# Cosine attention and a low-rank mixer MLP: buffer fills ahead of their loads, score bursts of two for one batch, one more PSUM bank

## The chip, the cores and the metric

The kernel runs on one core of a Trainium2 chip. The metric is the device time of one execution in microseconds (us). The kernel before takes 595.03 us, the median of three runs (594.52 to 596.84). The profiled execution that the views below describe has a span of 594.7 us.

## What is computed

Cosine attention over 8 batches, 12 heads, 448 tokens and 64 features per head, and then a mixer over each batch of 448 x 768: a low-rank mix along the tokens (rank 32), a residual, and an MLP from 768 to 3072 and back, with a second residual. In the reference, cut to what matters:

```python
q_n = q / (norm(q) + 1e-06);  k_n = k / (norm(k) + 1e-06)
scores = (q_n @ k_n.T) / tau
attn = softmax(scores)                      # over the keys
x = (attn @ v), heads side by side          # [8, 448, 768]
u = x + (x.transpose(0, 2, 1) @ U @ V).transpose(0, 2, 1)
out = u + relu(u @ w_ch1) @ w_ch2
```

## The kernel before, in words

**Stages of one batch.** Attention and MLP of all batches are woven into one stream. For each batch: GpSimd loads q and k in three thirds of four heads (`load_qk`, L490) and v (`load_v`, L510 for batches 0 to 2, L513 and L518 for the others). VectorE takes squares, sums and normalises (`stats`, `norm`, L540, L544, L612). The result xn is transposed to qkT: on the matrix engine (PE) for batches 0 and 1, by a transposing DMA from the sync queue for the others (L627). PE forms scores (`scores`, L670), ScalarE takes the exponential into attn (L688), PE multiplies with v (`values`, L713), and VectorE divides by the sum, which comes out of a column of ones beside v (L720, L722). `stage0` makes the low-rank mix (L768, L815) and adds it to X to give u (L829). u is transposed to uT (by DMA from batch 2 on, L849), and `mlp` runs the up product (L891), the relu (L914 on ScalarE or L916 on VectorE), the down product (L927), the residual (L938) and the store (L952).

**Buffers.** There are two v buffers, `v_t`, used by even and odd batches. Up to batch 2 (`b < WIDE`, 3) keys lie in four chunks of 112 rows; from batch 3 on in chunks of 128, with the last 64 keys of two pairs of heads sharing the 128 rows of the fourth chunk. So each v buffer has to be filled anew once, with ones beside v and zeros in the half that a head does not use: `set_v_tiles` (L976), five memsets on VectorE (L978, and L980 and L981 twice). `v_set[b]` holds that fill. It can start when the products with v of the batch that used the buffer before are done (`last_av`), and the products of the new batch wait for it. attn has three buffers, xn three, qkT six, u eight tiles, uT one, and the q/k tiles three.

**PSUM.** The eight banks are shared by rings, each with an ordered list of banks and a cap on how many it may hold: `r_sc` (scores, pairs of banks 0 to 5), `r_av` and `r_av2` (products with v), `r_low` (mixer products), `r_mm`, `r_up`, `r_out` (MLP products).

**Order.** A planner in the kernel's Python (`Plan`) simulates the five engines with a cost for each operation and writes out one fixed order for each engine. PE and GpSimd take operations from streams: PE prefers transposes, then products with v, the mixer, scores, and MLP products last; GpSimd has a single stream, so its loads keep the order in which they are written. VectorE, ScalarE and the sync queue take the ready operation with the lowest `prio`. DMAs have an estimated latency `lat`: a number, or a queue ("in" for loads, "x" for transposes) with a work and a fixed part. In the finished order each engine runs its instructions in turn and waits on semaphores where data or buffers demand it.

**Bursts.** `BURST[b]` says how many score slots (a pair of heads, a chunk of keys) of batch b are issued together. A burst of more than two slots is `big`: PSUM banks 0 to 5 are kept for it while it is next and its inputs are ready, and it is tied into the MLP of an earlier batch. Batch 2's big bursts are tied to the up products 0, 3, 6, ... 21 of batch 1; those of batch b from 3 on to down products of batch b - 2 (`SPOTS`). Batches 0 and 1 have no such ties. `BURST[b] > 2` also chooses the rings: `r_av2` rather than `r_av` in `values` (L708), `r_low` rather than `r_mm` in `stage0` (L758).

Of the kernel before, what the change touches and what calls it, by code (L numbers as in the profile page):

```python
# [269 lines left out]
def kernel(  # L270
# [14 lines left out]
    B, H, S, D = q.shape  # L285
# [3 lines left out]
    NPAIR = H // 2  # L289
# [7 lines left out]
    EPS = 1e-6  # L297
    PE_BATCHES = 2
    LATE, VLATE = 8.0, 2.8
    BURST = [1] + [2] * 1 + [3] * 6  # L300
    SPOTS = {8: [(6,)] * 7 + [()], 6: [(5, 17), (10,), (6,), (6,), (6,), (6,)]}
    WIDE = 3
    RAW_KEYS = {(0, 0), (0, 1), (0, 2), (0, 3)}
# [8 lines left out]
    def fixed(n, shape, dt, name):  # L312

        tiles = [const.tile(shape, dt, name=f"{name}{i}") for i in range(n)]
        return tiles
# [11 lines left out]
    v_t = fixed(2, [128, H, SC, D + 2], BF, "v_nat")  # L327
# [38 lines left out]
    def bank_ring(groups, cap, shape=None):  # L366
        def make(g):
            if len(g) > 1:
                return bank_t[:, g[0]:g[-1] + 1, :]
            t_ = bank_t[:, g[0], :]  # L370
            if shape is not None:
                t_ = t_[:, 0:shape[0] * shape[1]].rearrange("p (a b) -> p a b", a=shape[0])
            return t_
        return BankRing(banks, groups, cap, make)
# [2 lines left out]
    r_av = bank_ring([(5,), (6,), (7,), (4,)], 2, (4, D + 8))  # L377
    r_sc = bank_ring([(0, 1), (2, 3), (4, 5)], 3)
    r_low = bank_ring([(5,), (4,), (3,), (2,), (1,), (0,)], 2)
    r_av2 = bank_ring([(5,), (4,), (3,), (2,), (1,), (0,)], 2, (4, D + 8))  # L380
    r_up = bank_ring([(7,), (6,), (5,), (4,), (3,), (2,), (1,), (0,)], 4)
    r_out = bank_ring([(7,), (6,), (5,), (4,)], 4)
    r_warm = bank_ring([(4,)], 1)
# [18 lines left out]
    def rows(ap, c, s0, s1):  # L402

        return ap.rearrange("(s c) d -> c s d", c=SC)[c, s0:s1]
# [13 lines left out]
    def pe_t(n):  # L418
        return n / 2400.0 + 0.0025
# [4 lines left out]
    def dve_t(n, fast=1, fixed=0.065):  # L424
        return fixed + n * 0.00105 / fast
# [4 lines left out]
    def load(fn, busy, deps=(), acq=(), rel=(), late=2.0):  # L430
        return plan.add(Op("POOL", 0.71, fn, deps=deps, acq=acq, rel=rel,
                           lat=("in", busy, late)), pool_q)

    def fill(fn, n=256, prio=8, acq=(), deps=()):
        return plan.add(Op("DVE", 0.05 + n * 0.0005, fn, deps=deps, acq=acq, prio=prio))
# [47 lines left out]
    last_av = {}  # L483
# [12 lines left out]
    def key_rows(n0, n1):  # L496
        n = n0
        while n < n1:
            j, r = divmod(n, 128)
            c, s_ = divmod(n, SCH)  # L500
            m = min(n1 - n, 128 - r, SCH - s_)
            yield j, r, c, s_, s_ + m
            n += m

    def load_v(b):

        old = [last_av.get((b - 2, p)) for p in range(NPAIR)]
        src = v[b].rearrange("h (s c) d -> c s h d", c=SC)
        if b < WIDE:
            ops = [load(lambda c=c: nc.gpsimd.dma_start(out=v_t[b % 2][0:SCH, :, c, 0:D], in_=src[c]),  # L510
                        SCH * H * 0.001, deps=old, late=LATE if b else VLATE) for c in range(SC)]
        else:
            ops = [load(lambda j=j, r0=r0, c=c, s0=s0, s1=s1: nc.gpsimd.dma_start(  # L513
                out=v_t[b % 2][r0:r0 + s1 - s0, :, j, 0:D], in_=src[c, s0:s1]),
                (s1 - s0) * H * 0.001, deps=old, late=LATE) for j, r0, c, s0, s1 in key_rows(0, 384)]
            (_, _, c, s0, s1), = key_rows(384, S)
            for e, hh in ((0, 0), (0, 1), (1, 0), (1, 1)):
                ops.append(load(lambda e=e, hh=hh, c=c, s0=s0, s1=s1: nc.gpsimd.dma_start(  # L518
                    out=v_t[b % 2][64 * e:64 * e + 64, 2 * e + hh::4, SC - 1, 0:D],
                    in_=src[c, s0:s1, 2 * e + hh::4]),  # L520
                    (s1 - s0) * H * 0.00025, deps=old, late=LATE))
        for h in range(H):
            got[b, h, "v"] = ops
# [169 lines left out]
    def values(b, p, X):  # L693
# [12 lines left out]
        for hh in range(2):  # L706
            h = 2 * p + hh
            av, rd = Slot(r_av2 if BURST[b] > 2 else r_av, 1), Slot(r_rd, 1)  # L708
            for t in range(4):
# [46 lines left out]
    def stage0(b, X, muls):  # L756
        par = b % 2
        bank = r_sc1 if b == 1 else r_low if BURST[b] > 2 else r_mm  # L758
        by_pe = b < PE_BATCHES
# [110 lines left out]
    def mlp(b, us, uT, ut):  # L870
# [28 lines left out]
        for f in range(NC):  # L899
# [5 lines left out]
            if b == 0 and 9 <= f < 21 and f % 2:  # L905
                by_tokens(us, *state["first"], (f - 9) // 2)
            mm = early[f]
            o = up(f, mm, range(CC - 1, CC) if b == 0 and f < AHEAD else range(CC))
            r = Op("ACT/DVE", any_t(n), None, deps=[o], acq=[relu], rel=[mm],
                   prio=0)  # L910
# [10 lines left out]
        for group in groups:  # L921
            mms = [Slot(r_out if b == 0 else r_mm, 1) for _ in group]
            last, line = {}, []
            for f in range(NC):
                for (i, t, c0, c1), mm in zip(group, mms):
                    last[mm] = plan.add(Op("PE", pe_t(c1 - c0), lambda i=i, f=f, c0=c0, c1=c1, mm=mm:
                        nc.tensor.matmul(  # L927
                            out=mm.tile[:, 0:c1 - c0], lhsT=relu.tile[:, f, i * 128:(i + 1) * 128],
                            rhs=w2_t[:, f, c0:c1], start=(f == 0), stop=(f == NC - 1)),
                        deps=[done[f], w2_ops[f * len(w2_ops) // NC]],  # L930
                        acq=[mm] if f == 0 else [], rel=[relu] if f == NC - 1 else []), pe_mlp)
                    line.append(last[mm])
            downs.append(line)
            for (i, t, c0, c1), mm in zip(group, mms):
                w = c1 - c0
                O = Slot(r_O, 0)
                o = plan.add(Op("DVE", dve_t(w), lambda i=i, c0=c0, c1=c1, w=w, mm=mm, O=O:
                    nc.vector.tensor_add(out=O.tile[:, 0:w], in0=mm.tile[:, 0:w],  # L938
                                         in1=us[i].tile[:, c0:c1]),
                    deps=[last[mm]] + got.get((b, "u"), []), acq=[O], rel=[mm, us[i]], prio=1))  # L940
                for bb in (b - par, b - par + 1):
                    o0 = (bb % 2) * S
                    lo, hi = max(128 * t, o0), min(128 * (t + 1), o0 + S)
                    if lo >= hi:
                        continue
                    for nn, j, p0, p1 in segments(lo - o0, hi - o0):
                        r0 = nn + o0 - 128 * t
                        by = "ACT" if w < CH and p1 - p0 < SCH else "SP"
                        O.uses += 1
                        O.left += 1  # L950
                        plan.add(Op(by, 0.1, lambda bb=bb, j=j, p0=p0, p1=p1, r0=r0, O=O, c0=c0, c1=c1, by=by:
                            (nc.scalar if by == "ACT" else nc.sync).dma_start(  # L952
                                out=rows(out[bb], j, p0, p1)[:, c0:c1],
                                in_=O.tile[r0:r0 + p1 - p0, 0:c1 - c0]),
                            deps=[o], rel=[O], prio=2, lat=4.0))

        todo = bursts.get(b + 2, ()) if b else ()
        for o, f in zip(bursts.get(2, ()) if b == 1 else (), [0,3,6,9,12,15,18,21]):
# [17 lines left out]
    def set_v_tiles(t_):  # L976
        x = t_.rearrange("p (g e h) c d -> p g e h c d", e=2, h=2)
        nc.vector.memset(t_[:, :, 0:SC - 1, D:D + 2].bitcast(mybir.dt.uint32), ones)  # L978
        for e in range(2):
            nc.vector.memset(x[64 * e:64 * e + 64, :, e, :, SC - 1, D:D + 2].bitcast(mybir.dt.uint32), ones)  # L980
            nc.vector.memset(x[64 * e:64 * e + 64, :, 1 - e, :, SC - 1, :].bitcast(mybir.dt.uint32), 0)  # L981
# [33 lines left out]
    def groups_of(b):  # L1015
        if b < WIDE:
            slots = [(p, c) for p in range(NPAIR) for c in range(SC)]
            return [slots[n:n + BURST[b]] for n in range(0, len(slots), BURST[b])]
        slots = []
        for p in range(0, NPAIR, 2):  # L1020
            slots += [(p, 0), (p, 1), (p, 2), (p + 1, 0), (p + 1, 1), (p + 1, 2), (p, 3)]
        return [slots[n:n + BURST[b]] for n in range(0, len(slots), BURST[b])]

# [5 lines left out]
    def att(b):  # L1029
        X = Slot(r_X, 0) if b else X0  # L1030
        muls = [] if b else list(muls0)
        for x in groups_of(b) if b else ():
            scores(b, x)
        for p in range(0 if b else 1, NPAIR):
            if b == 0:
                for c in range(SC):
                    scores(b, [(p, c)])
            muls += values(b, p, X)
        if b < WIDE <= b + 2:
            v_set[b + 2] = [fill(lambda: set_v_tiles(v_t[b % 2]), 1200, prio=5, deps=[last_av[b, p] for p in range(NPAIR)])]  # L1040
        else:
            v_set[b + 2] = v_set[b]
        last_mul.extend(muls)
        return stage0(b, X, muls)
# [9 lines left out]
    v_set = {0: [fill(lambda: set_v(v_t[0]), 1000, prio=-1.4)]}  # L1054
    begun = stats_first(*first)
    X0 = Slot(r_X, 0)
    for c in range(SC):
# [7 lines left out]
                      deps=[zf, *begun], prio=-2, lat=12.0)) for t in range(4)]  # L1065
# [82 lines left out]
```

## Time and profile before

Busy time of three engines in stretches of the span, in us, with the clock that PE was granted, from the trace:

| stretch (us) | PE busy | VectorE busy | ScalarE busy | PE clock |
|---|---|---|---|---|
| 60 to 90 | 30.00 | 18.21 | 18.00 | 1.00 |
| 90 to 120 | 29.84 | 28.76 | 12.82 | 1.00 |
| 120 to 150 | 25.39 | 22.73 | 16.25 | 0.94 |
| 150 to 180 | 29.94 | 25.52 | 15.36 | 1.00 |
| 180 to 210 | 27.74 | 21.24 | 9.86 | 1.00 |
| 210 to 240 | 30.00 | 20.16 | 16.44 | 1.00 |
| 510 to 540 | 29.89 | 2.82 | 4.78 | 1.00 |

A stretch is 30 us long, so what is missing from 30 in the PE column is time in which no matmul ran. Attention work thins out to the right: VectorE is hardly busy near the end, where only MLP products are left. A row "waiter <- releaser: total, times, longest" in the view of waits says how long an engine stood before an instruction and what let it go; in a timeline the same stands in square brackets. Of the kernel's 384 score matmuls and 1536 products with v, those of batch 2 are found between 110 and 175 us.

### The profile page before, as it was taken

To read this page: it belongs to the slowest core of one execution; us is meant where nothing else is said; L and a number is where in the kernel's file an instruction comes from. 1 tells how busy PE (TensorE), PEld (TensorE's weight loads), DVE (VectorE), ACT (ScalarE), POOL (GpSimd) and SP (SyncE) were. 2 spreads that over 40 slices of the span, in tenths; PEclk is the share of its full clock that TensorE was granted. 3 is DMA by queue.
4 is the path that set the end of the run, shared out by engine and by line. 5 is a ranking of instruction groups with operands and counts; after the bars stand their busy time and mean duration, and the time that the engine had idled before them with its cause. 6 is when DMAs were issued, how large, how long until landed. Compare 5 with 4: busy or idle time off the path is not lost.

```text
span 594.7 us, 11669 instructions
## 1 busy us (share of the span) xinstructions
PE 577.5 (97%) x4860; PEld 329.2 (55%) x4878; DVE 300.9 (51%) x724; ACT 268.9 (45%) x445; POOL 89.8 (15%) x128
## 2 busy tenths in 40 slices
PE   7999999996999899999999999999999999999997
PEld 5555656543556565554456665654455666654565
DVE  7869849996986758466714671244202241110011
ACT  6977743563543364445454345335453444014300
POOL 8234220161024014013200040000000000000000
PEclk9999999998999999999999999999999999999999
DMA  9999992897739849356734690422021100310021
GB/s 155 199 207 192 209 138 69 136 106 88 116 41 165 102 63 109 90 107 79 62 67 83 102 99 21 105 59 45 0 55 41 40 15 1 94 40 1 1 53 54
DMA packets 133332, 50.68 MB, mean 85 GB/s; under 512 B 98208, under 2 KB 133280, under 8 KB 133280
## 3 DMA queue, kind: packets, MB, share of 16 engines
q0 software_dynamic: 72160, 25.73, 39.2%
q1 hardware_dynamic: 61056, 24.19, 20.0%
q8 instruction: 38, 0.62, 0.4%
q14 instruction: 14, 0.11, 0.1%
q10 hardware_dynamic: 64, 0.02, 0.0%
HBM read 52.25 MB, written 11.01 MB: 106 GB/s over the span
## 4 chain that ended last, share of the span: by engine, by line
PE 89%; DMA 4%; ACT 2%; DVE 2%; issue 1%; POOL 0%; DVEq 0%; ACTq 0%; POOLq 0%
PE bank L927 36%; PE bank L891 35%; PE bank L713 8%; PE bank L670 7%; DMA v_nat<-in_v_dram 2%; ACT attn L683 2%; PE bank L815 2%; DMA uT<-u_nat 1%; PE bank L468 1%; DMA qk_nat<-in_k_dram 1%; DVE xn L612 1%; PE bank L768 1%; DVE X_sb L722 0%; POOL qk_nat L490 0%; ACT sq L538 0%
## 5 line engine op out<-in xcount | busy, mean ns | idle before, releaser
L891 PE MATMUL bank<-uT,w_sb 128*128 128x384 bf16 (+1 forms) x1135 | 230.8, 353 | 8.3 <-DVE relu L916 4.3
L927 PE MATMUL bank<-w_sb,relu 128*128 128x384 bf16 (+1 forms) x1368 | 231.2, 323 | 0.0
L688 ACT ACTIVATE attn<-bank 128x896 bf16<-128x896 f32 (+1 forms) x161 | 137.1, 922 | 109.6 <-PE bank L670 109.5
L927 PEld LDWEIGHTS <-relu 128*128 128x128 bf16 x1368 | 128.4, 98 | 90.2 <-issue 12.3
L891 PEld LDWEIGHTS <-w_sb 128*128 128x128 bf16 x1152 | 109.7, 98 | 110.8 <-issue 16.2
L914 ACT ACTIVATE relu<-bank 128x384 bf16<-128x384 f32 (+1 forms) x164 | 88.8, 542 | 154.9 <-PE bank L891 153.5
L938 DVE TENSOR_TENSOR O_sb<-bank,u_nat 128x384 f32<-128x384 f32 (+1 forms) x57 | 31.0, 547 | 178.4 <-PE bank L927 156.3
L544 DVE TENSOR_REDUCE ss<-sq 112x8 f32<-112x512 bf16 x96 | 63.1, 673 | 1.3 <-ACT sq L538 1.1
L713 PEld LDWEIGHTS <-attn 128*128 128x128 bf16 (+1 forms) x1536 | 55.9, 98 | 10.2 <-issue 3.3
L713 PE MATMUL bank<-v_nat,attn 128*128 128x65 bf16 (+1 forms) x1536 | 58.9, 194 | 0.1
L612 DVE TENSOR_TENSOR xn<-qk_nat,inv 112x512 bf16<-112x512 bf16 x91 | 58.8, 682 | 0.2
L670 PE MATMUL bank<-qkT 64*128 64x448 bf16 (+1 forms) x384 | 52.6, 357 | 1.5 <-ACT qkT L966 0.6
L490 POOL DMA_DIRECT2D qk_nat<-in_q_dram x24 | 17.5, 728 | 196.6 <-DVE xn L612 155.8
L720 DVE RECIPROCAL rd<-bank 128x4 f32<-128x4 f32 x96 | 16.8, 176 | 51.7 <-PE bank L713 48.9
L722 DVE TENSOR_TENSOR X_sb<-bank,rd 128x256 bf16<-128x256 f32 x96 | 40.3, 420 | 2.3
L540 DVE TENSOR_TENSOR sq<-qk_nat 112x512 bf16<-112x512 bf16 x89 | 34.2, 412 | 0.0
L670 PEld LDWEIGHTS <-qkT 64*128 64x128 bf16 (+1 forms) x384 | 13.5, 95 | 27.9 <-issue 23.2
L916 DVE TENSOR_SCALAR relu<-bank 128x512 bf16<-128x512 f32 (+1 forms) x28 | 17.8, 635 | 21.1 <-PE bank L891 20.6
L513 POOL DMA_DIRECT2D v_nat<-in_v_dram x30 | 22.1, 745 | 41.6 <-PE bank L713 41.6
L829 DVE TENSOR_TENSOR u_nat<-bank,X_sb 128x384 bf16<-128x384 f32 (+2 forms) x45 | 22.2, 525 | 7.2 <-PE bank L815 7.0
L683 ACT ACTIVATE attn<-bank,inv 112x448 bf16<-112x448 f32 x32 | 17.4, 655 | 0.7 <-DVE inv L566 0.7
L490 POOL DMA_DIRECT2D qk_nat<-in_k_dram x24 | 16.9, 703 | 4.6 <-DMA w_sb<-in_moe_w_ch_dram 3.6
(58 smaller groups left out, 182.1 us busy)
## 6 DMA issues: line engine op xcount, KB each, us to landing
qk_nat<-in_q_dram POOLq DMA_DIRECT2D x23, 224.0 KB, 5.2
qk_nat<-in_k_dram POOLq DMA_DIRECT2D x23, 224.0 KB, 5.9
w_sb<-in_moe_w_ch_dram POOLq DMA_DIRECT2D x4, 1152.0 KB, 21.3
w_sb<-in_moe_w_ch_dram POOLq DMA_DIRECT2D x8, 576.0 KB, 16.0
v_nat<-in_v_dram POOLq DMA_DIRECT2D x17, 168.0 KB, 8.9
out_dram<-O_sb SPq DMA_DIRECT2D x15, 168.0 KB, 2.2
out_dram<-O_sb SPq DMA_DIRECT2D x16, 144.0 KB, 2.1
out_dram<-O_sb SPq DMA_DIRECT2D x16, 120.0 KB, 2.0
```

Of the source, the lines that this page charges most:

```text
L490: ops = [load(lambda i=i, src=src: nc.gpsimd.dma_start(out=ld.tile[:, i, lo:lo + h1 - h0, :], in_=src[b, h0:h1].rearrange("h (s c) d -> s ...
L540: nc.vector.tensor_mul(y, x, x)
L544: lambda i=i, a0=a0, a1=a1, sq=sq: nc.vector.reduce_sum(ss.tile[:, i, a0:a1, :].rearrange("p h c -> p (h c)"), sq.tile[:, 0:a1 - a0, :].re ...
L612: nc.vector.tensor_mul(dst, src, sc)
L670: nc.tensor.matmul(out=out, lhsT=qkT.tile.rearrange("p b s -> p (b s)")[r, n0:n0 + w], rhs=qkT.tile[r, SC:2 * SC, :].rearrange("p c s -> p ...
L688: exps.append(plan.add(Op("ACT", act_t(2 * S, 0.08), lambda sc=sc, c=c, attn=attn: nc.scalar.activation(out=attn.tile[0:SCH if b < WIDE el ...
L713: nc.tensor.matmul(out=av.tile[:, t, 0:D + 1], lhsT=(attn if j < SC - 1 else even).tile[0:kp, j, hh, 128 * t:128 * (t + 1)], rhs=v_t[b % 2 ...
L722: muls.append(plan.add(Op("DVE", dve_t(256), lambda av=av, rd=rd, h=h: nc.vector.tensor_mul(X.tile[:, :, h * D:(h + 1) * D], av.tile[:, :, ...
L891: o = plan.add(Op("PE", pe_t(n), lambda cc=cc: nc.tensor.matmul(out=mm.tile[:, 0:n], lhsT=w1_sb[:, cc, f * 128:(f + 1) * 128], rhs=uT.tile ...
L914: nc.scalar.activation(out=relu.tile[:, f, 0:n], in_=mm.tile[:, 0:n], func=AF.Relu)
L927: nc.tensor.matmul(out=mm.tile[:, 0:c1 - c0], lhsT=relu.tile[:, f, i * 128:(i + 1) * 128], rhs=w2_t[:, f, c0:c1], start=(f == 0), stop=(f ...
L938: nc.vector.tensor_add(out=O.tile[:, 0:w], in0=mm.tile[:, 0:w], in1=us[i].tile[:, c0:c1]),
```

## The change

Four edits, in five places:

1. The loads of v for batches 3 and 4 depend on the fill of their buffer, so that the fill comes first; its priority on VectorE goes from 5 to 3.5, ahead of the statistics (4). It is meant to keep VectorE from waiting for loads of the buffer it fills.
2. Batch 2 issues its scores two slots at a time. With that its bursts are no longer `big`: no ties to the up products of batch 1, no banks kept, and `r_av` and `r_mm` in place of `r_av2` and `r_low`.
3. Products with v of batches 3 to 7 may use bank 6 as a last choice.
4. The planner's latency of an output store is no longer a flat 4.0 but a share of the queue "x" and 2.0.

```diff
-    BURST = [1] + [2] * 1 + [3] * 6
+    BURST = [1] + [2] * 2 + [3] * 5
...
-    r_av2 = bank_ring([(5,), (4,), (3,), (2,), (1,), (0,)], 2, (4, D + 8))
+    r_av2 = bank_ring([(5,), (4,), (3,), (2,), (1,), (0,), (6,)], 2, (4, D + 8))
...
-        old = [last_av.get((b - 2, p)) for p in range(NPAIR)]
+        old = [last_av.get((b - 2, p)) for p in range(NPAIR)] + (v_set[b] if WIDE <= b < WIDE + 2 else [])
...
-                            deps=[o], rel=[O], prio=2, lat=4.0))
+                            deps=[o], rel=[O], prio=2, lat=("x", (p1 - p0) * w * 4 / 200e3, 2.0)))
...
-            v_set[b + 2] = [fill(lambda: set_v_tiles(v_t[b % 2]), 1200, prio=5, deps=[last_av[b, p] for p in range(NPAIR)])]
+            v_set[b + 2] = [fill(lambda: set_v_tiles(v_t[b % 2]), 1200, prio=3.5, deps=[last_av[b, p] for p in range(NPAIR)])]
```

## Prediction

> **What bounds the kernel now.** I read the page first: engines, then the 40 slices.
>
> ```profile
> span 594.7 us, 11669 instructions
> ...
> PE 577.5 (97%) x4860; PEld 329.2 (55%) x4878; DVE 300.9 (51%) x724; ACT 268.9 (45%) x445; POOL 89.8 (15%) x128
> ...
> PE   7999999996999899999999999999999999999997
> ```
>
> TensorE (PE) carries the span. It is not busy for 594.7 - 577.5 = 17.2 us. The change does not touch the arithmetic, so it can win only idle time, or time at a lowered clock. The slices show four thin places: the first and the last, which no edit reaches, the tenth (134 to 149 us) and the fourteenth (193 to 208 us). Next, the waits of PE, longest first:
>
> ```profile
> PE bank L891 <- DVE relu L916: 4.3, 1, 4.3
> PE bank L891 <- DMA uT<-u_nat: 2.3, 1, 2.3
> PE bank L598 <- DVE warm L987: 1.1, 1, 1.1
> ```
>
> Two single waits explain the two inner places; the third is the start. The timeline from 131 to 141 us shows the first:
>
> ```profile
> 132.95 0.09 DVE L978 MEMSET v_nat<- 128x36 uint32 x1
> 132.97 0.06 DVE L980 MEMSET v_nat<- 64x6 uint32 x1
> ...
> 133.42 1.69 PE L891 MATMUL bank<-uT,w_sb 128*128 128x512 bf16 x7
> ...
> 137.51 0.22 DVE L981 MEMSET v_nat<- 64x198 uint32 x1 [4.47 <-DMA v_nat<-in_v_dram]
> ...
> 138.71 0.68 DVE L916 TENSOR_SCALAR relu<-bank 128x512 bf16<-128x512 f32 x1
> ...
> 139.44 0.81 PE L891 MATMUL bank<-uT,w_sb 128*128 128x512 bf16 x3 [4.34 <-DVE relu L916]
> ```
>
> The fill of batch 3's v buffer stands on VectorE behind the loads of that buffer. Its zero fill (L981) sits 4.47 us until a v load has landed; behind it in VectorE's queue stand a square and then the relu that frees a PSUM bank, and PE waits 4.34 us for that relu. What follows is slow as well (stages of the trace; the clock is the field after the POOL count):
>
> ```profile
> 140.00:145.00 5.00, 4.78 (x44) 2.90 (x43) 4.96 (x13) 0.75 (x2) 0.00 (x0) 0.66 0.24 48
> 145.00:150.00 5.00, 5.00 (x54) 2.62 (x53) 3.15 (x7) 3.89 (x7) 1.39 (x2) 1.00 0.59 75
> 200.00:205.00 5.00, 4.74 (x80) 3.66 (x81) 3.46 (x12) 0.49 (x1) 0.00 (x0) 1.00 0.66 109
> ```
>
> Two pieces lie in the slow stretch: 32 products with v take 1.57 us instead of the usual 1.02, and 14 up products 4.06 instead of 14 x 0.219 = 3.07 (10.74 us for 49 in the chain, at 287.41). That is 0.55 + 0.99, about 1.6 us; 5 x (1 - 0.66) = 1.7 agrees. After the second wait the clock is 1.00, so it costs its length only. That second wait, in the chain of waits, and the same transposes by tile:
>
> ```profile
> 191.58 8.54 DMA uT<-u_nat
> 200.13 0.14 issue
> 200.26 1.46 PE bank L891 x8
> ```
>
> ```profile
> DMA to landing us min/median/max: 2.5/2.5/8.5
> ```
>
> Batch 2's last uT transpose was issued at 191.6, when only 6.1 us of down products were left, and took 8.5 us against a median of 2.5, between v and q/k loads and output stores.
>
> **What the Trainium skill says.** "TensorE: Matmul & The Clock Gate", Part 1, has the matrix clock fall to half after an idle window of about 3.4 us and recover after about as much work. The trace agrees: 4.34 us idle, then one-microsecond stages at 0.50 and all regained by 144; the 2.26 us wait cost no clock. The same page, on engine queue depths, calls VectorE strict FIFO; the relu held behind the memset shows it. "DMA: Bandwidth & Descriptors", Issuing engines are not separate DMA queues, says that transfers of all issuers interleave on the same 16 engines; the 8.5 us transpose fits that.
>
> **The change part by part.**
>
> *Fills ahead of the loads.* The loads of v for batches 3 and 4 now depend on the fill, and the fill's priority goes from 5 (behind the statistics, 4) to 3.5. Batch 1's last products with v end near 97 us, while the fill ran at 133: it had stood behind statistics all that time. Now it runs soon after 97 and costs VectorE what it did: 0.09 + 2 x 0.06 + 2 x 0.22 = 0.65 us. The new wait is on GpSimd. Behind those v loads stand the q/k loads of batch 4 in its queue, and batch 4's statistics wait for these. But v(3) is issued at 124.97, after q/k loads that wait for the xn products, so the fill is some 25 us early and the wait is hidden. For batch 4 the fill already ran at 175.0, as its loads began (174.90): at most 0.7 us on loads that batch 4's products with v need some 50 us later. Gain: 4.34 us of idle and 1.6 us of clock, 5.9 in all.
>
> *Batch 2 in bursts of two.* 12 bursts in place of 8, the same matmuls. Two bursts in the chain:
>
> ```profile
> 49.23 0.48 PE bank L670 x4
> ```
>
> ```profile
> 115.42 0.67 PE bank L670 x6
> ```
>
> 12 x 0.48 - 8 x 0.67 = +0.4 us on PE, on the path. The larger effect is order. A burst of two is not "big": batch 2's bursts lose the ties to the up products of batch 1, and no banks are kept for them. Its products with v and its first mixer products get bank lists with banks 6 and 7 in them. In the trace these bursts run from 110.7 to 157.5 and the last products with v at 173.5, although xn of the last pairs was ready at 123.3 and a qkT transpose lands in 4.0 us. Untied, the scores can end near 135 and products with v near 145; the last transpose then follows at the distance seen (173.5 to 191.6, 18 us), near 163. The one uT buffer is free when batch 1's up products end, near 149 with the first wait gone. uT is needed near 192: 29 us of slack, in which 8.5 us of transposing is hidden. Gain: 2.3 us. PE loses nothing by doing attention work earlier: MLP products fill the rest, and the last 110 us (after the last product with v at 482) are MLP alone already.
>
> *A seventh bank* (bank 6, last choice) for products with v of batches 3 to 7. These batches show no wait of PE of note: 330 us from 240 to 570 hold 0.7 us of idle in the stage table. Nothing to gain: 0. The *output stores' latency* changes only the planner's estimate, from a flat 4.0 to a share of the queue that the transposes use; a store lands in about 2 us either way. The output is stored while PE has 3 buffers' worth of down products ahead: 0.
>
> Sum: 595.0 - 4.3 - 1.6 - 2.3 + 0.4 = 587.2.
>
> **The rivals.**
>
> B: *uT still late.* The tie goes but the wait stays, or one of its size opens elsewhere: batch 2's chain may be held by VectorE, busy 28.8 of 30 us from 90 to 120, or by the three attn buffers. For it: the transpose's 8.5 us is contention, and earlier v(4) loads move that, not end it. Against: the 29 us of slack. 595.0 - 5.9 + 0.4 = 589.5.
>
> C: *a new wait in the new order.* Both old waits go but untied bursts come to the head of PE's in-order queue before qkT has landed, or a relu stands behind softmax exponentials on ScalarE. A qkT transpose took 2.9 to 8.3 us to land: a burst planned on the median could wait some 4.3 us, cold clock after it 1.6: 587.2 + 5.9 = 593.1. Against: batch 1's bursts of two were untied too, and PE idled only 0.2 us from 60 to 120. Batch 2's transposes, though, are made by DMA where batch 1's are made on PE.
>
> D: *slower.* The second wait stays and two such stalls open: 589.5 + 2 x 5.9 = 601.3. For it: the whole order after 97 us is planned anew, on estimated landing times, and the 8.5 us transpose shows how far one can be off. Against: scores and products with v of five later batches show no such stall.
>
> **How the numbers follow.** My case A 0.50, B 0.27, C 0.15, D 0.06, and 0.02 for better than A. The likeliest is A, 587.2. The range goes from 585.8 (A with the bursts' 0.4 hidden and the other inner idle, about 1 us, gone too) to 593.0, which takes in B and about half of C. Faster by over 0.5% means below 592.05: A, B, the 0.02 and a third of C give 0.84. Within 0.5% (to 598.0): the rest of C and a little of D, 0.11. Slower: 0.05.
>
> **What would show it.** Fills: the five memsets run near 97 us, none with a DMA before it, and no PE idle near 135; the clock stays 1.00 there. Bursts: L670 groups of four between 100 and 140, and batch 2's uT transposes before 165 with the first up product of batch 2 not idle before. Bank 6: no change in idle from 240 on. Wrong would be: PE waits of over 1 us on qkT, attn or relu between 95 and 205, or a clock below 1.00 there; then C or D. A memset that still waits for a load would undo the largest step.

## The result, and the profile after

The kernel after takes 588.54 us (median of four runs, 588.29 to 589.45), the kernel before 595.52 in the runs beside it: a ratio of 0.9884, 95% interval 0.9861 to 0.9908. It is faster by 7.0 us. The forecast was 587.2, with a range of 585.8 to 593.0. One execution of the experiment gap_t below, the profiled one, ran at a lowered clock from its start to its end; it is left out, and no trace of that kernel is read.

The page of the kernel after, the lines that answer to those shown of before:

```profile
span 586.5 us, 11699 instructions
...
PE 578.0 (99%) x4878; PEld 328.0 (56%) x4878; DVE 301.7 (51%) x725; ACT 268.6 (46%) x444; POOL 89.8 (15%) x128
...
PE   7999999999999999999999999999999999999997
```

The two thin places inside the span are gone; those at the ends are left. The waits of PE, longest first:

```profile
PE bank L598 <- DVE warm L987: 1.1, 1, 1.1
PE bank L468 <- DVE xn L612: 0.9, 2, 0.5
PE bank L670 <- ACT qkT L966: 0.6, 1, 0.6
PE bank L891 <- ACT uT L966: 0.6, 1, 0.6
```

All of these belong to the first 42 us. Neither the relu (4.3) nor the uT transpose (2.3) is in the list any more. The timeline of VectorE shows where the fill of batch 3's buffer went:

```profile
101.04 0.09 DVE L978 MEMSET v_nat<- 128x36 uint32 x1
101.06 0.06 DVE L980 MEMSET v_nat<- 64x6 uint32 x1
101.09 0.22 DVE L981 MEMSET v_nat<- 64x198 uint32 x1
101.36 0.06 DVE L980 MEMSET v_nat<- 64x6 uint32 x1
101.41 0.22 DVE L981 MEMSET v_nat<- 64x198 uint32 x1
```

It runs 0.6 us long at 101, without a wait, 25 us ahead of the first load of that buffer (125.7). Stages of the trace around the old gap and around the old uT wait, with the PE clock as the field after the POOL count:

```profile
135.00:140.00 5.00, 5.00 (x27) 2.02 (x26) 4.54 (x10) 4.46 (x8) 0.80 (x2) 1.00 1.47 169
140.00:145.00 5.00, 5.00 (x55) 2.35 (x54) 4.67 (x12) 3.36 (x5) 1.40 (x2) 1.00 0.64 98
190.00:195.00 5.00, 5.00 (x64) 3.48 (x62) 2.93 (x9) 1.42 (x4) 0.00 (x0) 1.00 0.60 127
```

PE is busy throughout and at full clock. The sync queue issues batch 2's uT transposes like this, and the first up product of that batch follows:

```profile
174.62 1.22 SPq L849 DMA_TRANSPOSE uT<-u_nat  x1
...
179.11 3.35 SPq L849 DMA_TRANSPOSE uT<-u_nat  x2
```

```profile
192.84 2.11 PE L891 MATMUL bank<-uT,w_sb 128*128 128x384 bf16 x12
```

The last of them is issued by 182.5, some 10 us before it is needed; in the kernel before it was issued by 192.8, some 5 us before PE was ready for it at 198.0.

So much for what is gone. It does not yet say which of the edits took it away: that was the question for the chip.

### The profile page after: what moved, and what is told of

Its sections match the earlier page's. It is cut to its first block, busy times and chain, and to the rows that moved or that the text cites. A ratio compares the mean times of both kernels' runs of the same rounds, so it can differ in the third digit from the quotient of the medians.

```text
span 586.5 us, 11699 instructions
## 1 busy us (share of the span) xinstructions
PE 578.0 (99%) x4878; PEld 328.0 (56%) x4878; DVE 301.7 (51%) x725; ACT 268.6 (46%) x444; POOL 89.8 (15%) x128
## 4 chain that ended last, share of the span: by engine, by line
PE 94%; ACT 3%; DVE 2%; DMA 0%; issue 0%
PE bank L927 38%; PE bank L891 37%; PE bank L713 8%; PE bank L670 7%; ACT attn L683 2%; PE bank L815 2%; PE bank L468 1%; PE bank L768 1%; ACT sq L538 1%; DMA raw_uv<-in_q_dram 0%; DVE xn L612 0%; DVE ss L544 0%; DVE u_nat L829 0%; ACT qkT L966 0%; PE bank L749 0%
## 5 line engine op out<-in xcount | busy, mean ns | idle before, releaser
L891 PE MATMUL bank<-uT,w_sb 128*128 128x512 bf16 (+1 forms) x1152 | 233.2, 353 | 0.6 <-ACT uT L966 0.6
L914 ACT ACTIVATE relu<-bank 128x384 bf16<-128x384 f32 (+1 forms) x161 | 87.0, 541 | 142.6 <-PE bank L891 142.2
L916 DVE TENSOR_SCALAR relu<-bank 128x512 bf16<-128x512 f32 (+1 forms) x31 | 19.8, 638 | 13.9 <-PE bank L891 13.7
```

Of the source, the lines that this page charges most:

```text
L891: o = plan.add(Op("PE", pe_t(n), lambda cc=cc: nc.tensor.matmul(out=mm.tile[:, 0:n], lhsT=w1_sb[:, cc, f * 128:(f + 1) * 128], rhs=uT.tile ...
L914: nc.scalar.activation(out=relu.tile[:, f, 0:n], in_=mm.tile[:, 0:n], func=AF.Relu)
```

## Experiments

Theory at the start: the fill edit removes the first wait and its clock dip (5.9 us), the bursts of two remove the uT wait (2.3 us) and cost 0.4, and the other two edits do nothing. The rival: it is the new order as a whole, not the place of the fill.

### Each edit alone, on the kernel before

**o_fill**, the fill edit:

```diff
-        old = [last_av.get((b - 2, p)) for p in range(NPAIR)]
+        old = [last_av.get((b - 2, p)) for p in range(NPAIR)] + (v_set[b] if WIDE <= b < WIDE + 2 else [])
...
-            v_set[b + 2] = [fill(lambda: set_v_tiles(v_t[b % 2]), 1200, prio=5, deps=[last_av[b, p] for p in range(NPAIR)])]
+            v_set[b + 2] = [fill(lambda: set_v_tiles(v_t[b % 2]), 1200, prio=3.5, deps=[last_av[b, p] for p in range(NPAIR)])]
```

> The kernel before with the fill edit alone (loads of v depend on the fill, priority 3.5). Theory (two separate waits, each edit removes its own): the 4.3 us wait of PE near 135 us and the clock dip after it go, the wait for batch 2's uT near 198 us stays at 2 to 3 us; span 594.7 - 5.9 = 588.8, ratio to before about 0.990. Rival (the new order of batch 2 is what helps, the fill only moves its wait to GpSimd's loads): no more than 1 us gained, ratio 0.998 or more.

Measured: 589.11 us, ratio 0.9905 (0.9886 to 0.9924). The time is as expected, but the uT wait did not stay at 2 to 3 us. The waits of PE have it at

```profile
PE bank L891 <- DMA uT<-u_nat: 0.5, 1, 0.5
PE bank L891 <- DVE relu L916: 0.2, 1, 0.2
```

and the bursts of batch 2 are still tied and still of three.

**o_burst**, the bursts alone:

```diff
-    BURST = [1] + [2] * 1 + [3] * 6
+    BURST = [1] + [2] * 2 + [3] * 5
```

> The kernel before with batch 2 in bursts of two alone. In the order that results, both fills stand behind loads of their own buffer on VectorE (the one for batch 3 in part, the one for batch 4 with both zero fills). Theory: the uT wait goes (-2.3) and the bursts cost 0.4, but VectorE still waits for v loads, of batch 4 now, some 4 to 9 us, and PE behind it 3 to 6 us with a cold clock after; ratio 0.996 to 1.008. Rival (the bursts carry the gain): ratio 0.987 to 0.990.

Measured: 589.75 us, ratio 0.9918 (0.9898 to 0.9939): near the rival's number, a miss for the theory. The fills do stand behind their loads in VectorE's order, both buffers one after the other, but the timeline shows them without a wait:

```profile
171.41 0.09 DVE L978 MEMSET v_nat<- 128x36 uint32 x1
171.44 0.06 DVE L980 MEMSET v_nat<- 64x6 uint32 x1
171.47 0.22 DVE L981 MEMSET v_nat<- 64x198 uint32 x1
...
172.17 0.22 DVE L981 MEMSET v_nat<- 64x198 uint32 x1
```

At priority 5 the fill is put off until VectorE has nothing better to do; in this order that is at 171, when the loads, whose last is issued at 163.5, have landed. So the bursts remove the same wait as the fill edit, from the other side: the fill runs late enough instead of early enough.

**o_bank**, bank 6 for `r_av2` alone, and **o_lat**, the planner's latency of the stores alone:

```diff
-    r_av2 = bank_ring([(5,), (4,), (3,), (2,), (1,), (0,)], 2, (4, D + 8))
+    r_av2 = bank_ring([(5,), (4,), (3,), (2,), (1,), (0,), (6,)], 2, (4, D + 8))
```

> The kernel before with the seventh bank for products with v alone. Theory: nothing before batch 3 changes, both waits stay; span 594.7 within 1 us, ratio 0.998 to 1.002. Rival (PSUM banks hold products with v back): ratio below 0.997.

Measured: 593.76 us (20 runs), ratio 0.9978 (0.9965 to 0.9991), about 1.2 us faster than before: a small miss for the theory. The fill still waits for its loads (4.1 us at most), and PE behind it:

```profile
140.83 4.84 PE L891 MATMUL bank<-uT,w_sb 128*128 128x512 bf16 x15 [3.10 <-DVE relu L916]
```

The expectation that nothing before batch 3 changes was wrong. In the kernel before, batch 2 still has bursts of three, and so takes the banks for its products with v from `r_av2` as well (L708): alone, this edit reaches batch 2. VectorE's order differs from that of before from 130 us on, while batch 3's products with v start only at 178. The 32 products with v that came after the old wait now run ahead of it, PE waits 3.1 us instead of 4.3, and the uT transposes are issued by 184.8 for a product at 199.1, so that there is no uT wait.

```diff
-                            deps=[o], rel=[O], prio=2, lat=4.0))
+                            deps=[o], rel=[O], prio=2, lat=("x", (p1 - p0) * w * 4 / 200e3, 2.0)))
```

> The kernel before with the planner's latency of the output stores changed alone. In the order that results the fill of batch 3's buffer happens to stand ahead of its loads, with no edit to the fill. Theory (what counts is where the fill stands, not which edit puts it there): the wait near 135 us is gone with its clock dip, the uT wait stays or changes by its own; ratio about 0.990 (0.986 to 0.993). Rival (a planner estimate cannot matter, as I predicted 0 for this edit): ratio 0.998 to 1.002 with the 4.3 us wait in place.

Measured: 589.14 us, ratio 0.9904 (0.9888 to 0.992). An edit that touches no instruction, only an estimate, brings as much as the fill edit: the order it leads to has the fill at 122.0, ahead of the loads, which are issued from 125.6 on. The uT wait is still there, though the view names VectorE as its end:

```profile
192.74 1.62 PE L891 MATMUL bank<-uT,w_sb 128*128 128x384 bf16 x9 [0.84 <-DVE ln L564]
```

The last uT transpose, issued at 185.9, took 6.7 us and so landed at 192.6, just ahead of this product. Three edits out of four, each alone, bring 5.2 to 5.8 us. They cannot be added: they remove the same wait.

### The wait itself, with nothing moved

**o_split** keeps the order of before on every engine and writes each zero fill as two memsets, one for each head of a pair, so that it no longer waits for loads into the neighbouring heads' rows:

```diff
-            nc.vector.memset(x[64 * e:64 * e + 64, :, 1 - e, :, SC - 1, :].bitcast(mybir.dt.uint32), 0)
+            for hh in range(2):
+                nc.vector.memset(x[64 * e:64 * e + 64, :, 1 - e, hh, SC - 1, :].bitcast(mybir.dt.uint32), 0)
```

> The kernel before in its own order on every engine, but each of the two zero fills of set_v_tiles written as two memsets (one for each head of a pair), so that no memset of batch 3's buffer waits for a load any more. Nothing is moved. Theory (the wait of VectorE for v loads is the whole of the first gap): no PE wait of over 0.5 us near 135 us, clock 1.00 there, ratio 0.988 to 0.992, and what is left of the uT wait near 195 us shows whether it was a consequence of the first. Rival (the gain comes from the new order, and something else, such as qkT or attn, ends last once the fill is out of the way): PE idles some 2 to 4 us at the same place for another reason, ratio 0.995 or more.

Measured: 588.44 us (587.43 to 591.64), ratio 0.9906 (0.9869 to 0.9943). VectorE at the place of the old wait:

```profile
132.31 0.09 DVE L978 MEMSET v_nat<- 128x36 uint32 x1
132.34 0.06 DVE L980 MEMSET v_nat<- 64x6 uint32 x1
132.35 0.25 DVE L982 MEMSET v_nat<- 64x99 uint32 x2
132.65 0.06 DVE L980 MEMSET v_nat<- 64x6 uint32 x1
132.68 0.25 DVE L982 MEMSET v_nat<- 64x99 uint32 x2
132.96 0.43 DVE L540 TENSOR_TENSOR sq<-qk_nat 112x512 bf16<-112x512 bf16 x1
133.30 0.68 DVE L916 TENSOR_SCALAR relu<-bank 128x512 bf16<-128x512 f32 x1
```

The relu that stood at 138.7 is at 133.3, and no other wait of PE takes its place. No new order is needed, and the fill may stay in the middle of its loads: the data never called for the wait. The zero fill and the loads write different heads' rows, interleaved in the same partitions; the one memset over both heads was made to wait for loads into rows between its own, the two narrower ones are not. This run speaks against the rival. The uT wait is gone here too, but barely: the transposes are issued by 185.7 for a product at 191.3, as tight as before, and the last one, started at 183.75, took 7.5 us and landed 0.1 us ahead of that product.

**a_late** does the reverse on the kernel after: the fill is planned right behind the issue of its last load.

```diff
+        if WIDE <= b < WIDE + 2:
+            sent = plan.add(Op("POOL", 0.0, lambda: None), pool_q)
+            v_set[b] = [fill(lambda: set_v_tiles(v_t[b % 2]), 1200, prio=-1, deps=[sent])]
         for h in range(H):
             got[b, h, "v"] = ops
...
-        if b < WIDE <= b + 2:
-            v_set[b + 2] = [fill(lambda: set_v_tiles(v_t[b % 2]), 1200, prio=3.5, deps=[last_av[b, p] for p in range(NPAIR)])]
-        else:
+        if not b < WIDE <= b + 2:
```

The dependence of the loads on the fill is taken out as well.

> The kernel after with the fills put behind the issue of their loads on purpose (priority -1 as soon as the last v load is issued), the other edits kept. Theory: VectorE waits for loads in flight again, 4 to 8 us for batch 3's buffer and as much for batch 4's; PE idles behind it one or two times, with a clock dip where it idles over about 3 us; ratio to before 0.995 to 1.008, that is 4 to 12 us slower than after. Rival (bursts of two hide the wait): ratio below 0.991.

Measured: 593.34 us (592.84 to 593.63), ratio 0.9967 (0.9956 to 0.9979), 4.8 us slower than after. The wait of VectorE is back for both buffers, 8.2 us in four pieces; the longest (L984 is the zero fill here, L930 the down product, L941 the residual):

```profile
169.36 0.22 DVE L984 MEMSET v_nat<- 64x198 uint32 x1 [4.70 <-DMA v_nat<-in_v_dram]
```

```profile
171.29 1.14 PE L930 MATMUL bank<-w_sb,relu 128*128 128x384 bf16 x6 [1.82 <-DVE O_sb L941]
```

PE stands only 1.8 us right behind the wait of 4.7, where it is a residual that is queued behind the fill and not a relu. That is not the whole price: three shorter waits of PE follow the two fills (0.7 us for a relu and 0.6 for X at 135 to 137, 1.0 for attn before 176.5), 4.1 us in all of the 4.8; that the fills cause these three is likely, not shown. The clock stays at 1.00. How much a wait on VectorE costs depends on what is queued behind it.

### What an idle of PE costs in clock

**gap_t, gap_s, gap_l** put three, five and eight copies that nobody reads on ScalarE, ahead of one relu of the last batch, where only the MLP runs:

```diff
+            lag = 5 if b == B - 1 and f == 8 else 0
...
-            def fn(r=r, f=f, mm=mm):
+            def fn(r=r, f=f, mm=mm, lag=lag):
+                for _ in range(lag):
+                    nc.scalar.copy(out=attn_t[0][:, 0:2, 0, :], in_=attn_t[1][:, 0:2, 0, :])
```

> The kernel after with five idle copies of 1024 columns (attn to attn, read by nobody) on ScalarE ahead of the relu of up product 8 of the last batch, some 5.2 us. By then only the MLP runs. PE should stand about 2 us there. Theory (a short idle of PE costs its length, no clock): about 590.5 us, clock 1.00 in the 5 us after it. Rival (every idle of some us costs clock): 592.

> The same with eight copies, some 8.3 us; PE should stand about 5 us. Theory (an idle of over 3 to 4 us halves the clock for some 3 to 4 us): about 588.5 + 5.2 + 1.6 = 595.3 us, a stretch of clock near 0.5 after the idle. Rival (the dip in the kernel before had another cause, such as the mix of shapes): 593.7, clock 1.00.

> The kernel after with three idle copies on ScalarE before the relu of up product 8 of the last batch. Five copies (5.3 us) left PE idle 3.8 us and eight left it idle 7.1, so three should leave it idle about 1.7 us. Theory (such an idle is too short to lower the clock): 588.5 + 1.7 = 590.2 us, clock 1.00 after it, a spread of under 2 us. Rival (the clock falls with a chance that grows with the idle): some executions near 592.4 with a clock of 0.997.

I had guessed too much slack: five copies left PE idle 3.8 us, not 2, so gap_s did not test a short idle; gap_t was added for that. Stages of one microsecond of gap_s after its idle (534.4 to 538.2):

```profile
537.00:538.00 1.00, 0.00 (x0) 0.00 (x0) 0.00 (x0) 1.00 (x2) 0.00 (x0) 0.98 0.00 0
538.00:539.00 1.00, 0.80 (x2) 0.25 (x2) 0.00 (x0) 0.63 (x2) 0.00 (x0) 0.50 0.00 0
539.00:540.00 1.00, 1.00 (x4) 0.44 (x3) 0.00 (x0) 0.00 (x0) 0.00 (x0) 0.50 0.00 0
540.00:541.00 1.00, 1.00 (x4) 0.30 (x3) 0.00 (x0) 0.05 (x1) 0.00 (x0) 0.50 0.00 0
541.00:542.00 1.00, 1.00 (x5) 0.44 (x4) 0.00 (x0) 0.55 (x1) 0.00 (x0) 0.81 0.00 0
```

Times by the mean granted clock of each execution, against 588.7 us for after:

| kernel | PE idle (trace) | clock 0.999 to 1.000 | clock 0.996 to 0.997 | clock 0.991 to 0.994 |
|---|---|---|---|---|
| gap_t | not read | 590.5 to 591.1 (3) | none | none |
| gap_s | 3.8 | 592.4 (2) | 594.6 (11) | 595.5 (7) |
| gap_l | 7.1 | none | none | 598.0 (4) |
| before | 4.3 | none | 594.4 (28) | 595.7 (28) |
| o_bank | 3.1 | 592.4 (4) | 593.7 (11) | 595.2 (5) |

(Means, or the span where it says "to", with the number of executions in brackets; the idle is that of the one profiled execution. The base of 588.7 is that of the three gap kernels alone.) The clock falls in pieces of one length: the stages of gap_s above lose 0.02 + 3 x 0.50 + 0.19 = 1.71 us of clock, which is 3.4 us at half, and those of gap_l lose 3.41 us in one stretch, twice as much. Over a span of some 594 us this makes a mean clock of 0.997 and 0.994. By this estimate the three columns hold executions with no such piece, with one, and with two or three. gap_s explains itself: 588.7 + 3.8 = 592.5 is the time of the two executions in which the clock did not fall; where it fell, the same idle cost another 2.2 or 3.1 us. gap_l: 588.7 + 7.1 = 595.8, and 2.2 on top on average (1.3 to 2.8). That is no more than one piece cost in gap_s, because in gap_l's trace some 2 us of the first piece fall within the idle itself. gap_t: 1.8 to 2.4 us longer than after, and no clock in any of the three. So a longer idle costs clock more often, with a spread that the prediction did not have: the same idle of 3.8 us can cost nothing or 3 us of clock.

The Trainium skill ("TensorE: Matmul & The Clock Gate", Part 1) says that the window in which activity is judged is about 3.4 us long and runs freely; the pieces of 3.4 us agree with that. Its other statement, which the prediction took over, that the clock falls after an idle window of this length, does not fit: in o_bank's trace an idle of 3.1 us was enough.

```profile
139.00:140.00 1.00, 0.00 (x0) 0.00 (x0) 1.00 (x3) 0.00 (x0) 0.00 (x0) 1.00 0.54 76
140.00:141.00 1.00, 0.17 (x1) 0.10 (x1) 1.00 (x3) 0.00 (x0) 0.00 (x0) 0.68 0.00 0
141.00:142.00 1.00, 1.00 (x3) 0.30 (x2) 1.00 (x4) 0.00 (x0) 0.00 (x0) 0.50 0.00 0
142.00:143.00 1.00, 1.00 (x4) 0.39 (x3) 1.00 (x4) 0.00 (x0) 0.00 (x0) 0.50 0.33 66
143.00:144.00 1.00, 1.00 (x5) 0.33 (x4) 1.00 (x3) 0.41 (x1) 0.00 (x0) 0.61 0.85 163
```

And by an estimate from the page's 3.4 us, a freely running window would lie wholly within an idle of 3.8 us in about one execution of eight ((3.8 - 3.4) / 3.4), where 18 of 20 lost clock. In the trace of before, a stage of 0.69 from 140 to 141 means that the clock fell at about 140.4, when PE had been busy again for 0.9 us. The measurement decides: the clock was kept after 2.3 us of idle (the uT wait in the trace of before) and fell after 3.1 us. What exactly is judged stays open.

The clock is also a part of why the kernel before spreads from 593.2 to 598.4 us and the kernel after from 588.3 to 589.5. None of the 56 executions of before in the table kept its clock above 0.997; of the eight of after and after_again below, six did, and the other two are the slowest (589.45 and 589.41).

### The change less one edit

On one chip, beside **after_again**, the kernel after once more.

> The kernel after once more, on the chip of the three runs that follow, to compare them with. 588.5 us, spread of under 2 us, clock 0.999 to 1.000 in every execution, against about 4 us of spread for the kernel before.

Measured: 588.74 us (588.66 to 589.41), ratio 0.9899 (0.9877 to 0.9922).

**a_noburst**, all but the bursts of two:

```diff
-    BURST = [1] + [2] * 2 + [3] * 5
+    BURST = [1] + [2] * 1 + [3] * 6
```

> The kernel after with batch 2 in bursts of three again, all other edits kept. My prediction gave the bursts 2.3 - 0.4 = 1.9 us of the gain: 590.4. Theory now (the wait for uT was a late landing in one execution, and any one edit that keeps the fill off the loads has the whole gain): within 1 us of after, the uT transposes issued only some 6 us before they are needed, an idle of PE there of 0 to 1 us.

Measured: 587.68 us (587.58 to 588.04), ratio 0.988 (0.9858 to 0.9902). This beats both kernels: its slowest execution is 0.6 us below the fastest of after_again. No PE wait for uT, and its transposes are issued by 176.4 for a product at 194.3, with more room than in the kernel after. With the other edits in place the bursts of two, and the rings that go with them, bring nothing and cost 1.1 us. Most of it is to be seen in the group of score matmuls, first of after_again, then of a_noburst:

```profile
L670 PE MATMUL bank<-qkT 64*128 64x448 bf16 (+1 forms) x384 | 53.3, 357 | 1.3 <-ACT qkT L966 0.6 <-ACT attn L683 0.4
```

```profile
L670 PE MATMUL bank<-qkT 64*128 64x448 bf16 (+1 forms) x384 | 52.6, 357 | 1.5 <-ACT qkT L966 0.6 <-ACT attn L683 0.5
```

The same 384 matmuls are busy 0.7 us longer when they come in four more groups. The other 0.4 us was not located.

**a_nofill**, all but the fill edit:

```diff
-        old = [last_av.get((b - 2, p)) for p in range(NPAIR)] + (v_set[b] if WIDE <= b < WIDE + 2 else [])
+        old = [last_av.get((b - 2, p)) for p in range(NPAIR)]
...
-            v_set[b + 2] = [fill(lambda: set_v_tiles(v_t[b % 2]), 1200, prio=3.5, deps=[last_av[b, p] for p in range(NPAIR)])]
+            v_set[b + 2] = [fill(lambda: set_v_tiles(v_t[b % 2]), 1200, prio=5, deps=[last_av[b, p] for p in range(NPAIR)])]
```

> The kernel after without the fill edit, all others kept. In this order the fills stand behind their loads on VectorE, but late. Theory (a fill behind its loads costs only while they are in flight; as with the bursts alone, they have landed by then): within 1.5 us of after, no wait of VectorE for v loads. Rival (what stands behind a load always waits): 593, as where the fills were put right behind the loads.

Measured: 588.69 us (588.65 to 588.72), ratio 0.9896 (0.987 to 0.9922), the time of after. Both fills run from 171.7 to 173.0 us without a wait. With the other edits in place, either the fill edit or the bursts can be left out without bringing the wait back. What the change is without bank 6, or without the stores' latency, was not measured.

## Why the prediction was right, and where its steps were not

**The first wait and its clock: right.** VectorE's queue, held by a fill that waits for loads, was the cause: o_split removes that wait with nothing moved and has 6.3 of the 7.0 us (3.4 to 7.8 by its interval; the trace has no uT wait either). The size of the clock term, 1.6 us, was that of one execution; for an idle of about this length, in gap_s, it was 0 to 3.

**The fill hidden on GpSimd: right.** The fill ran at 101 (forecast: soon after 97), and the loads of 125.7 did not wait for it. For batch 4 it ran at 154.0, its loads from 154.9.

**The uT wait: gone as forecast, but the gain was not the bursts'.** The step that did not hold is "Untied, the scores can end near 135 ... Gain: 2.3 us", the assignment of this gain to the bursts. With tied bursts of three, o_split, o_bank and a_noburst have no such wait, o_fill has 0.5 us of it and o_lat 0.8. It was no fixed cost but a margin near nothing: PE had 6.4 us of work left when the last transpose was issued (down products and a group of scores; the 6.1 us of the prediction is a little short), and in before, o_split, o_lat and o_fill that transpose took 8.5, 7.5, 6.7 and 6.1 us. The profiled execution of before, 596.7 us at a clock of 0.997, is 2.3 us longer than the mean of the 28 executions at 0.996 to 0.997 (594.4). This suggests, and no second trace of before shows, that most of them wait less for uT than that one did. The bursts do move the transposes forward as forecast (in o_burst they are issued by 171.2 for a product at 194.2), but a_noburst has them by 176.4 without them. The estimate of where the chain would be was off too: scores of batch 2 ended at 148 (forecast 135), the last uT transpose was issued by 182.5 (forecast 163), so that 10 us of the 29 us of slack were there. Why the mixer products of batch 2 start only at 169.7, when the last products with v ended at 153, was not settled; it costs nothing.

**The bursts' own cost: too small.** 0.4 us forecast, 1.1 measured, of which 0.7 was found in the score matmuls.

**Bank 6: forecast 0; alone it measured 0.9978, about 1.2 us.** Alone it acts on batch 2, as o_bank showed, and the first wait of PE is 1.2 us shorter there (3.1 against 4.3). That this is the whole of it is not shown. In the change as it is batch 2 uses `r_av`, so that the edit acts on batches 3 to 7 only, as the prediction said; its effect there was not measured.

**The stores' latency: "0" failed as a step.** I priced the stores and not the order that the estimate leads to; alone it moves the fill and brings 5.8 us. In the sum it changed nothing, since the same wait had been counted once.

**The base of the sum.** The terms were read from an execution of 596.7 us and taken from the median, 595.0. From its own execution the sum is 596.7 - 7.8 = 588.9, against 588.5 measured with that profile. The base makes a difference of 1.7 us, more than the 1.3 us by which the forecast was too low. That the sum of this one execution comes so close is in part luck: it takes the whole uT wait off, which others may not have, and too little for the bursts. By the two traces: 594.7 - 586.5 = 8.2 us, against 4.3 + 2.3 + 1.6 - 0.7 for the scores, and 0.8 from the start, where no edit acts (the products with v that begin at 95.92 begin at 95.13).

Of the rivals, none came: no new wait of PE opened between 95 and 205 us.

## What to carry to other kernels

When an engine that runs in order waits for a transfer, ask first whether the bytes call for it: here a narrower access pattern of the same memset removed the wait with no change of order and brought most of the gain (6.3 of 7.0 us). Edits that remove the same wait do not add up, so measure each alone and each left out before keeping one that has a cost of its own, as the bursts of two had. And take a sum of trace terms off the time of the execution that the trace is of, not off a median.

## What the runs showed that was not expected

- An estimate in a planner, with no instruction changed, was worth 5.8 us (ratio 0.9904), by moving one fill from the middle of its loads to ahead of them.
- The same idle of 3.8 us cost 0, about 2 or about 3 us of clock from one execution to the next (592.4, 594.6, 595.5). The clock fell in pieces of 3.4 us, and an idle of 3.1 us could already bring one (o_bank).
- A fill behind loads in flight cost PE 4.3 us where a relu was queued behind it, and 1.8 us where a residual was, though VectorE waited 4.5 and 4.7. With the shorter waits that followed, the second still cost 4.8 us of time.
- A list of PSUM banks for later batches also acted on batch 2, because the burst size chooses the list (o_bank, ratio 0.9978).
